# FFN products at full array width, and the first batch's outputs stored by SyncE from the accumulators' buffers

## The chip, the cores and the metric

The kernel runs on one core of a Trainium2 chip. A core has a matrix engine (TensorE, PE in the profile; its weight loads have a row of their own, PEld), three engines for element-wise work (VectorE or DVE, ScalarE or ACT, GpSimd or POOL), and SyncE (SP), which only issues transfers. ACT and POOL issue transfers as well. Each engine works through its own list of instructions in order; engines wait for each other, and for transfers, by semaphores.

The metric is the device time of one execution in microseconds. Seven executions of the kernel before lie between 547.52 and 553.15 us, with a median of 549.8 us.

## What is computed

Attention with squared ReLU in place of softmax, followed by a layer norm and a two-layer feed-forward part (FFN) with a residual:

```python
scores = scale * np.matmul(q, k.transpose(0, 1, 3, 2))      # q, k, v: 8 batches, 12 heads, 448 tokens, 64
attn = np.maximum(scores, 0.0) ** 2 / S
attn_out = np.matmul(attn, v)
x = attn_out.transpose(0, 2, 1, 3).reshape(B, S, H * D)      # 8 x 448 x 768
xn = (x - mu) / np.sqrt(var + 1e-06) * g_ln
ch = np.maximum(xn @ w_ch1, 0.0) @ w_ch2                    # 768 -> 3072 -> 768
out = x + ch
```

## The kernel before

**Order of the work.** All instructions are issued in an order that is written out by hand; nothing reorders them. Batch 0's attention comes first, in fine steps (step_fine, L531). Then, for each batch b, FFN 1 (ffn_1_all, L587) and FFN 2 (ffn_2_first, L616, for batch 0, and ffn_2_all, L642, for the others). The attention of batch b + 1 is spread over the FFN of batch b: in batch 0 by step_a and step_b, later in groups called excursions (L513): one attention value product if one is due, then two or three score products with their ReLU and square, and then the FFN goes on.

**Products.** A matmul has a stationary side of up to 128 columns and a moving side. Scores (L225) contract over the 64 elements of a head, two heads in the two halves of the array's rows. The value product (att_AV, L250) has 64 stationary columns a head and puts two heads into the two halves of the array's columns, as the transposes of batches 0 and 1 (pe_T, L189) do. Their stationary sides are shown as 64*112, 112*64 and 112*64.

FFN 1 (ffn_1, L317) makes 128 of the 3072 hidden features at a time for a batch's 448 tokens: six contraction steps, each of which is two matmuls of 64 stationary columns (128*64), one for either half of the columns. Only the first three feature tiles of batch 0 (ffn_1_first, L568, matmuls on L574) use 128 columns at once. Results go to two PSUM banks in turn (next_f), and ACT writes their ReLU to h (L324). FFN 2 of batch 0 (plain_part, L358) takes two token tiles of 128 and two halves of 384 output features, each in four parts of six contraction steps; every step is again a pair of 64-column matmuls (L367). FFN 2 of the other batches (seven, L395) makes two token tiles at a time with seven products of half size (Strassen's way), by product (L381, matmuls on L384), from sums of pieces of h (s_sb, L378) and of w2 (w2_sums, L174). center (L278) takes the mean of x by a matmul with constants, in pairs as well (L282).

**Around batch 0's FFN 2.** Between its sixteen parts ACT scales x of batch 1 by the gains (gain, L276), DVE subtracts the mean (center_part, L288), copies the tokens left over to the next batch (carry, L333) and makes sums of w2 (L176). After a tile's last part DVE adds the residual (scaled_plus, L353) into a buffer of o_pool (new_o, three buffers), and the result is stored. store (L339) makes two transfers of one tile, as a tile's 128 tokens cross a boundary of 112 in the output's layout. It takes the issuing engines as an argument: SP if none is named, and for batch 0 ACT. The other batches' outputs are in buffers of o_pool and of acc_pool (four buffers, tag "acc"), and SP stores them.

**SP's list.** SP also issues the transposes of q and k for the batches from 2 on (att_T, L202: two for each pair of heads; three pairs' results fit into t_pool) and the transposes of x into x_tok, tokens on the rows (ffn_x, L300). At the end of batch 0 its list is: six transposes of q and k (pairs 12 to 14), then twelve of x for batch 1, with those of pair 15 after the sixth and of pair 16 after the twelfth.

Of the kernel before, what the change touches and what calls it, by code (L numbers as in the profile page):

```python
# [11 lines left out]
def kernel(  # L12
# [10 lines left out]
    nc = tc.nc  # L23
    P = 128
    bf16 = mybir.dt.bfloat16
    fp32 = mybir.dt.float32
# [3 lines left out]
    B, H, S, D = q.shape  # L30
# [8 lines left out]
    K1 = d_model // P  # L39
    K2 = d_ff // P  # L40
    KH = K2 // 2
    HD = d_model // 2
# [14 lines left out]
    acc_pool = ctx.enter_context(tc.tile_pool(name="acc", bufs=4))  # L57
# [9 lines left out]
    ones = const_pool.tile([P, P], bf16)  # L67
# [5 lines left out]
    w1 = big_pool.tile([P, K1, d_ff], bf16)  # L73

    w2 = big_pool.tile([P, 7, KH, HD], bf16)
    B11, B22, B12, B21, B_SUM, B_TOP, B_BOT = range(7)
    h = big_pool.tile([P, K2, HW], bf16)
# [3 lines left out]
    xc = big_pool.tile([P, K1, S], bf16)  # L81
# [158 lines left out]
    def xT_of(b, ki):  # L240
        return xT[:, ki, (b % 2) * S:(b % 2 + 1) * S]
# [36 lines left out]
    def center(b):  # L278
        mean_ps = spare[1][:, :S]
        for n, part in enumerate((xs, xT_of(b, K1 - 1))):  # L280
            for c in range(2):
                nc.tensor.matmul(mean_ps[c * D:(c + 1) * D, :], ones[:, :D], part,  # L282
                                 start=(n == 0), stop=(n == 1))
        for ki in range(K1):
            center_part(ki, mean_ps)

    def center_part(ki, mean_ps):
        nc.vector.scalar_tensor_tensor(xc[:, ki, :], mean_ps, g_sb[:, ki:ki + 1], xc[:, ki, :],  # L288
                                       op0=Alu.mult, op1=Alu.add)
# [27 lines left out]
    def ffn_1(ni):  # L317
        ps = next_f()[:, :S]
        for ki in range(K1):
            for c in range(2):  # L320
                n0 = ni * P + c * D
                nc.tensor.matmul(ps[c * D:(c + 1) * D, :], w1[:, ki, n0:n0 + D], xc[:, ki, :],  # L322
                                 start=(ki == 0), stop=(ki == K1 - 1))
        nc.scalar.activation(h[:, ni, CARRY:], ps, Act.Relu)  # L324

    def h_cols(b, m):
        c0 = CARRY + m * P - b * S
        return slice(c0, c0 + P)
# [6 lines left out]
    def new_o():  # L335
        o_t = o_pool.tile([P, HD], fp32, tag="o")
        return o_t

    def store(o_t, m, d0, d1, engines=(nc.sync,)):  # L339
        c0 = m * P  # L340
        n = 0
        while c0 < (m + 1) * P:
            g0 = c0 // SP
            c1 = min((m + 1) * P, (g0 + 1) * SP)
            bb, jj = divmod(g0, NJ)
            engines[n % len(engines)].dma_start(
                out_tok[bb, c0 - g0 * SP:c1 - g0 * SP, jj, d0:d1],
                o_t[c0 - m * P:c1 - m * P, :d1 - d0])
            c0 = c1
            n += 1  # L350

    def scaled_plus(o_t, y, m, plus):
        nc.vector.scalar_tensor_tensor(o_t, y, rstd[:, m:m + 1], plus, op0=Alu.mult, op1=Alu.add)  # L353

    def x_half(m, dh):
        return x_tok[:, m % NT, dh * HD:(dh + 1) * HD]

    def plain_part(b, m, dh, part, parts, box):  # L358
        if part == 0:
            box[0] = next_f()[:, :HD]  # L360
        n = K2 // parts
        cols = h_cols(b, m)
        for ki in range(part * n, (part + 1) * n):
            slot = ((B11, B12), (B21, B22))[ki // KH][dh]
            for c in range(2):
                t0 = cols.start + c * D
                nc.tensor.matmul(box[0][c * D:(c + 1) * D, :], h[:, ki, t0:t0 + D],  # L367
                                 w2[:, slot, ki % KH, :], start=(ki == 0), stop=(ki == K2 - 1))
        if part == parts - 1:
            o_t = new_o()  # L370
            scaled_plus(o_t, box[0], m, x_half(m, dh))
            store(o_t, m, dh * HD, (dh + 1) * HD, (nc.scalar,))

    s_turn = Turns(range(4))

# [4 lines left out]

    def product(ps, stat, slot, start, d0=0, d1=HD):  # L381
        for ki in range(KH):
            for c in range(2):
                nc.tensor.matmul(ps[c * D:(c + 1) * D, :d1 - d0], stat[:, ki, c * D:(c + 1) * D],  # L384
                                 w2[:, slot, ki, d0:d1],
                                 start=(start and ki == 0), stop=(ki == KH - 1),
                                 skip_group_check=not start)

    posts = []

# [4 lines left out]
    def seven(b, pair, banks, last, between):  # L395
# [43 lines left out]
        def s(name, x, y, op):  # L439
# [3 lines left out]

        steps = [
            (lambda: product(c, a11, B12, True), s(1, a11, a22, Alu.add), after3),
            (lambda: product(d, a22, B21, True), s(5, a11, a12, Alu.add), after4),
            (lambda: product(a, sums[1], B_SUM, True), s(2, a21, a22, Alu.add), after1),
            (lambda: product(c, sums[5], B22, False), s(7, a12, a22, Alu.subtract), after5),
            (lambda: product(d, sums[2], B11, False), s(6, a21, a11, Alu.subtract), after2),
# [137 lines left out]
    def ffn_1_all(b):  # L587
        steps = second_steps() if b == 0 else None
        ms = tiles_of(b)
        for ni in range(3 if b == 0 else 0, K2):  # L590
            if b == 0 and ni == 3:
                ffn_1_first()
            if 3 <= ni < 3 + K1:
                ffn_x(b, ni - 3)
            ffn_1(ni)
            flush()
            m = (ni - (K2 - 2 * len(ms))) // 2
            if m >= 0 and ni % 2 == 0:
                ffn_stats(ms[m])
            if b == 1 and ni in SUMS_AT:  # L600
                w2_sums(*LATE_SUMS[SUMS_AT.index(ni)])
            if b == 0 and ni % 2 == 1:
                next(steps)()
            if 0 < b < B - 1 and ni in IN_FFN1[b]:
                excursion(3, relus=(2,))
        assert steps is None or next(steps, None) is None
# [9 lines left out]
    def ffn_2_first():  # L616
        b = 0
        ffn_rstd(b)
        box = {}
        n = 0  # L620
        for dh in range(2):
            for m in range(2):
                for part in range(4):
                    plain_part(b, m, dh, part, 4, box)
                    if n == 1:
                        att_AV(PE_T * NPAIR - 1, bank=spare[0])
                    if n < K1 - 1:
                        gain(1, n)
                    if n == 3:
                        gain(1, K1 - 1)  # L630
                    if n == 4:
                        gain(1, K1 - 2)
                        center(1)
                    if n == 8:
                        carry(b)
                    if n in (9, 10):
                        w2_sums(B_SUM, B11, B22, Alu.add, n - 9)
                    if n in (12, 13):
                        w2_sums(B_TOP, B11, B12, Alu.add, n - 12)
                    n += 1  # L640

    def ffn_2_all(b):  # L642
# [9 lines left out]
        def between(n):  # L652
            n += 7 * (pr - first)
            if n == (8 if len(pairs) == 2 else 1):
                carry(b)
            if b == B - 1:
                return
            if slots_left():
                if n in (1, 3):
                    excursion(min(2, slots_left()), av_bank, nc.scalar, square_by=nc.scalar)  # L660
            elif ready:
                att_AV(ready.pop(0), bank=av_bank, evac_by=nc.scalar)
            done = (b + 2) * NPAIR - len(ready) - NPAIR * (b + 1)
            done -= sum(1 for i, t in slots if t == NJ - 1 and i < (b + 2) * NPAIR)
            if not gains and not centered[0]:
                center(b + 1)
                centered[0] = True
            for _ in range(2):
                if gains and gains[0] < done:
                    gain(b + 1, gains.pop(0))  # L670
# [75 lines left out]
```

## Time and profile before

One execution was profiled. It took 552.49 us; its span, from the first to the last instruction, is 550.6 us.

| | before |
|---|---|
| median of seven executions | 549.8 us |
| the profiled execution | 552.49 us |
| its span | 550.6 us |
| instructions | 13785 |
| matmuls, and as many weight loads | 5729 |
| FFN 1 matmuls in pairs (L322) | 2268, of 448 columns |
| FFN 2 matmuls in pairs (L384, L367) | 2208 and 192, mostly of 384 columns |
| granted TensorE clock, mean | 0.994 |

A row of the profile's groups names the line, engine and operation, then what is written and read, the stationary side (128*64: 128 rows, 64 columns), the moving side, the count, the busy time and the mean duration, and last the idle time of the engine before the group with what ended it. Matmuls overlap: a matmul of 448 columns is shown 350 to 355 ns long, while the next one can start about 190 ns after it, so the time of a stream is read from starts. In the timeline a row is "start, duration, engine, line", with equal instructions joined, and in brackets how long the engine was idle ahead of it and what ended that. The row PEclk gives the granted clock in 40 slices of 13.8 us each.

### The profile page before, as it was taken

Reading aid. Unit: us, or ns where it says so; the run is one execution under the profiler, and the core shown is the slowest. Engines: PE = TensorE matmul, PEld = TensorE weight load, DVE = VectorE, ACT = ScalarE, POOL = GpSimd, SP = SyncE. Lnnn points to the kernel's source line nnn. Section 1 sums busy time; section 2 is a strip of 40 time slices with the busy share of each in tenths; the row PEclk is TensorE's granted clock in tenths of the full one; section 3 lists DMA queues with packets and bytes.
Section 4 is the critical chain, followed back from the end, with each engine's and each line's share of the span. In section 5 each row is a group of like instructions: output and inputs, shape, how many; then the busy total and the mean of one; then the engine's idle time right before and its main releaser. Section 6 shows DMA issues by size and latency. Waiting matters only on the chain. (4 is left out here: it accounts for less than half of the span.)

```text
span 550.6 us, 13785 instructions
## 1 busy us (share of the span) xinstructions
PE 528.9 (96%) x5729; PEld 342.6 (62%) x5729; DVE 369.4 (67%) x660; ACT 306.6 (56%) x487; POOL 205.0 (37%) x261
## 2 busy tenths in 40 slices
PE   7999997799999999999999999999999999999996
PEld 4445565355786556855578556654578556787785
DVE  4975668499584785757866679766866678740464
ACT  6957741565816666266662765376562766524421
POOL 7421137036444642445524438224815200240021
PEclk9999999799999999999999999999999999999999
DMA  9999999669536984269942789258942820122022
GB/s 153 195 188 207 204 170 149 87 88 107 63 67 105 113 83 69 62 104 108 94 69 64 79 91 133 54 85 87 125 69 73 92 35 3 30 79 57 11 59 59
DMA packets 163022, 51.87 MB, mean 94 GB/s; under 512 B 128784, under 2 KB 162960, under 8 KB 162960
## 3 DMA queue, kind: packets, MB, share of 16 engines
q0 software_dynamic: 94208, 25.74, 48.2%
q1 hardware_dynamic: 67616, 24.07, 24.0%
q10 hardware_dynamic: 1136, 1.19, 0.7%
q8 instruction: 45, 0.74, 0.6%
q14 instruction: 17, 0.14, 0.1%
HBM read 51.91 MB, written 11.01 MB: 114 GB/s over the span
## 5 line engine op out<-in xcount | busy, mean ns | idle before, releaser
L322 PE MATMUL f<-xc,w 128*64 128x448 bf16 x2268 | 227.7, 355 | 6.2 <-ACT h L324 3.3
L322 PEld LDWEIGHTS <-w 128*64 128x64 bf16 x2268 | 131.1, 110 | 94.9 <-issue 23.7
L324 ACT ACTIVATE h<-f 128x448 bf16<-128x448 f32 x189 | 103.0, 545 | 100.5 <-PE f L322 86.4
L231 ACT ACTIVATE at<-sc 112x896 bf16<-112x896 f32 x149 | 128.3, 916 | 16.1 <-PE sc L225 15.9
L384 PE MATMUL f<-w,s_sb 128*64 128x384 bf16 (+2 forms) x1584 | 132.6, 324 | 1.2 <-DVE s_sb L378 1.2
L384 PEld LDWEIGHTS <-s_sb 128*64 128x64 bf16 x1584 | 103.8, 110 | 25.8 <-issue 2.7
L236 DVE TENSOR_TENSOR at<-at 112x896 bf16<-112x896 bf16 x177 | 100.9, 618 | 7.6 <-ACT at L231 7.4
L136 POOL DMA_DIRECT2D qk_ring<-in_q_dram x72 | 50.8, 711 | 112.0 <-DMA qkT_t<-qk_ring 91.7
L418 POOL TENSOR_TENSOR o_t<-o_t,x_tok 128x384 f32<-128x384 f32 x26 | 23.8, 914 | 138.9 <-ACT o_t L417 84.9
L229 DVE TENSOR_SCALAR at<-f 112x448 bf16<-112x448 f32 x86 | 49.5, 617 | 35.9 <-PE f L225 35.9
L378 DVE TENSOR_TENSOR s_sb<-h 128x1536 bf16<-128x1536 bf16 x65 | 63.3, 991 | 0.0
L136 POOL DMA_DIRECT2D qk_ring<-in_k_dram x72 | 50.3, 703 | 18.8 <-DMA w<-in_moe_w_ch_dram 12.4
L384 PE MATMUL f<-w,h 128*64 128x384 bf16 x624 | 54.3, 326 | 2.3 <-DVE acc L432 1.8
L418 POOL TENSOR_TENSOR acc<-acc,x_tok 128x384 f32<-128x384 f32 x25 | 35.8, 1442 | 42.4 <-ACT acc L417 42.4
L384 PEld LDWEIGHTS <-h 128*64 128x64 bf16 x624 | 40.9, 110 | 13.6 <-issue 3.8
L225 PE MATMUL sc<-qkT_t 64*112 64x448 bf16 x298 | 47.0, 378 | 1.5 <-DMA qkT_t<-qk_ring 1.2
L417 ACT ACTIVATE o_t<-f,rstd 128x384 f32<-128x384 f32 x26 | 14.9, 575 | 54.7 <-DVE acc L422 38.0
L260 DVE TENSOR_SCALAR xT<-f 128x448 bf16<-128x448 f32 x37 | 22.8, 617 | 30.2 <-PE f L250 20.6
L288 DVE SCALAR_TENSOR_TENSOR xc<-f,g_sb,xc 128x448 bf16<-128x448 f32 x48 | 29.3, 677 | 19.3 <-PE f L282 15.0
L250 PE MATMUL f<-at,v_ring 112*64 112x448 bf16 x336 | 41.0, 354 | 0.1
L225 PEld LDWEIGHTS <-qkT_t 64*112 64x112 bf16 x384 | 20.1, 126 | 33.4 <-issue 26.9
L417 ACT ACTIVATE acc<-acc,rstd 128x384 f32<-128x384 f32 x25 | 14.8, 610 | 34.8 <-DVE acc L432 33.4
(65 smaller groups left out, 342.6 us busy)
## 6 DMA issues: line engine op xcount, KB each, us to landing
w<-in_moe_w_ch_dram POOLq DMA_DIRECT2D x6, 768.0 KB, 27.7
w<-in_moe_w_ch_dram POOLq DMA_DIRECT2D x4, 1152.0 KB, 36.5
qk_ring<-in_q_dram POOLq DMA_DIRECT2D x72, 56.0 KB, 3.4
qk_ring<-in_k_dram POOLq DMA_DIRECT2D x72, 56.0 KB, 3.9
v_ring<-in_v_dram POOLq DMA_DIRECT2D x36, 112.0 KB, 4.0
out_dram<-o_t SPq DMA_DIRECT2D x7, 168.0 KB, 2.2
x_tok<-xT SPq DMA_TRANSPOSE x72, 3.6
qkT_t<-qk_ring SPq DMA_TRANSPOSE x72, 3.3
```

The lines of the kernel that those rows point to most:

```text
L136: nc.gpsimd.dma_start(sb[:, :, x, :], src[b, 2 * a + x].rearrange("(p j) d -> p j d", j=NJ))
L225: nc.tensor.matmul(half[:SP, :S], qkT[i][r, 1, t * SP:(t + 1) * SP], qkT[i][r, 0, :], start=True, stop=True)
L229: nc.vector.tensor_scalar(at[:, hh], spare[hh][:SP, :S], 0.0, None, op0=Alu.max)
L231: nc.scalar.activation(at, ps[:SP, :, :S], Act.Relu)
L236: nc.vector.tensor_mul(attn[i, t], attn[i, t], attn[i, t])
L250: nc.tensor.matmul(ps[hh * D:(hh + 1) * D, :], v_of(i)[:, hh, t * D:(t + 1) * D], attn[i, t][:, hh, :], start=(t == 0), stop=(t == NJ - 1))
L322: nc.tensor.matmul(ps[c * D:(c + 1) * D, :], w1[:, ki, n0:n0 + D], xc[:, ki, :], start=(ki == 0), stop=(ki == K1 - 1))
L324: nc.scalar.activation(h[:, ni, CARRY:], ps, Act.Relu)
L378: nc.vector.tensor_tensor(s_sb[:, n], x, y, op=op)
L384: nc.tensor.matmul(ps[c * D:(c + 1) * D, :d1 - d0], stat[:, ki, c * D:(c + 1) * D], w2[:, slot, ki, d0:d1], start=(start and ki == 0), sto ...
L417: nc.scalar.activation(o_t, y, Act.Identity, scale=rstd[:, m:m + 1])
L418: nc.gpsimd.tensor_tensor(o_t, o_t, x_half(m, dh), op=Alu.add)
```

## The change

There are two parts. The FFN products and the mean of center run with 128 stationary columns in one matmul where two matmuls of 64 stood. Batch 0's four output tiles are put into acc_pool's buffers in place of o_pool's, and are stored by SP in place of ACT. On SP the eight stores then stand after the six transposes of pairs 12 to 14 and before those of x for batch 1.

```diff
 def center(b):
     mean_ps = spare[1][:, :S]
     for n, part in enumerate((xs, xT_of(b, K1 - 1))):
-            for c in range(2):
-                nc.tensor.matmul(mean_ps[c * D:(c + 1) * D, :], ones[:, :D], part,
-                                 start=(n == 0), stop=(n == 1))
+            nc.tensor.matmul(mean_ps, ones, part, start=(n == 0), stop=(n == 1))
...
 def ffn_1(ni):
     ps = next_f()[:, :S]
     for ki in range(K1):
-            for c in range(2):
-                n0 = ni * P + c * D
-                nc.tensor.matmul(ps[c * D:(c + 1) * D, :], w1[:, ki, n0:n0 + D], xc[:, ki, :],
-                                 start=(ki == 0), stop=(ki == K1 - 1))
+            nc.tensor.matmul(ps, w1[:, ki, ni * P:(ni + 1) * P], xc[:, ki, :],
+                             start=(ki == 0), stop=(ki == K1 - 1))
...
 def plain_part(b, m, dh, part, parts, box):
...
-            for c in range(2):
-                t0 = cols.start + c * D
-                nc.tensor.matmul(box[0][c * D:(c + 1) * D, :], h[:, ki, t0:t0 + D],
-                                 w2[:, slot, ki % KH, :], start=(ki == 0), stop=(ki == K2 - 1))
+            nc.tensor.matmul(box[0], h[:, ki, cols], w2[:, slot, ki % KH, :],
+                             start=(ki == 0), stop=(ki == K2 - 1))
         if part == parts - 1:
-            o_t = new_o()
+            o_t = acc_pool.tile([P, HD], fp32, tag="acc")
             scaled_plus(o_t, box[0], m, x_half(m, dh))
-            store(o_t, m, dh * HD, (dh + 1) * HD, (nc.scalar,))
+            store(o_t, m, dh * HD, (dh + 1) * HD)
...
 def product(ps, stat, slot, start, d0=0, d1=HD):
     for ki in range(KH):
-            for c in range(2):
-                nc.tensor.matmul(ps[c * D:(c + 1) * D, :d1 - d0], stat[:, ki, c * D:(c + 1) * D],
-                                 w2[:, slot, ki, d0:d1],
-                                 start=(start and ki == 0), stop=(ki == KH - 1),
-                                 skip_group_check=not start)
+            nc.tensor.matmul(ps[:, :d1 - d0], stat[:, ki], w2[:, slot, ki, d0:d1],
+                             start=(start and ki == 0), stop=(ki == KH - 1),
+                             skip_group_check=not start)
```

## The prediction

> **What bounds the kernel now.** I read the page's busy shares and clock row first, then the chain of waits that ended last, then the waits of 70 to 125 us, then the timeline there.
>
> ```profile
> PE 528.9 (96%) x5729; PEld 342.6 (62%) x5729; DVE 369.4 (67%) x660; ACT 306.6 (56%) x487; POOL 205.0 (37%) x261
> ...
>
> ```
>
> ```profile
> 491.13 27.24 PE f L322 x288
> ```
>
> TensorE is the bound: 528.9 of 550.6 us busy, and the last chain is nearly all matmuls. The second fence is one piece of that chain: 288 matmuls of 64 columns are 144 pairs in 27.24 us, so **189.2 ns a pair** of 448 columns. Two halves run beside each other; a pair is not two times 189 ns. So almost every time that I remove from TensorE counts, and almost nothing that I remove elsewhere. One clock digit is not 9: slice 7 (96 to 110 us).
>
> ```profile
> ACT h L324 <- DMA out_dram<-o_t: 13.4, 1, 13.4
> ...
> ACT xc L276 <- DMA qkT_t<-qk_ring: 7.8, 1, 7.8
> ...
> PE f L322 <- ACT h L324: 3.3, 1, 3.3
> ```
>
> ```profile
> 87.67 4.09 PE L367 MATMUL f<-w,h 128*64 128x384 bf16 x48 [1.97 <-DVE o_t L353]
> ...
> 95.16 1.33 PE L322 MATMUL f<-xc,w 128*64 128x448 bf16 x12 [1.74 <-DVE o_t L353]
> ...
> 99.22 0.98 ACT L324 ACTIVATE h<-f 128x448 bf16<-128x448 f32 x2 [13.44 <-DMA out_dram<-o_t]
> 99.81 2.45 PE L322 MATMUL f<-xc,w 128*64 128x448 bf16 x12 [3.32 <-ACT h L324]
> ...
> 102.20 0.99 PE L225 MATMUL sc<-qkT_t 64*112 64x448 bf16 x4
> ```
>
> The first of these two fences is the table of waits in that window (who waited <- for what: us, times, longest), the second the timeline. Eight stores of batch 0 are issued by ACT (L372). ACT works in order, so a store whose wait isn't over holds everything behind it. The second store waits, by the semaphore it carries, for an earlier DMA of the same semaphore, one of SP's transposes; ACT's gains (L276) stand behind it for 7.8 us. DVE's centring waits for these gains, and the second output (L353) stands behind the centring; PE needs its bank: 1.97 us. The other stores hold ACT until 99.22, so that the first ReLUs of batch 1 are 13.4 us late: 3.32 us of PE.
>
> **Part 1: the stores go to SP.** What the stall costs. PE idle is 1.97 + 0.34 (at 92.10) + 1.74 + 3.32 = 7.37 us. A matmul's row ends some 0.16 us after the next could have started (350 ns long at a pitch of 189), so each of the four gaps in the stream is longer by that: +0.65. After the last gap the clock is low: the windows give 0.58 for 96 to 100 us and 0.56 for 100 to 104. There 12 matmuls take 2.45 us that take 1.33 at 95.16 (+1.1), and the scores that start at 102.20 are followed by FFN work at 103.49, 1.29 us later, where the next such group takes 0.70 (107.02 to 107.72): +0.6. Sum 9.7 us. (The Trainium skill, "TensorE: Matmul & The Clock Gate", section "Why this matters for your kernels", has the clock fall after a PE gap of some 3 us; the 3.32 us gap with 0.56 after it agrees, so without the gap the digit should be 9.)
>
> What is late next. With ACT free, its six gains are done by 77.6 us and the centring runs 78.98 to 82.7 (six at 0.62). Then DVE in its order: second output 0.6 (to 83.4), carry 1.45, two weight sums 2.6, third output 0.6 (88.0), two sums 2.6, fourth output (91.2). PE with no gap ends the sixteen parts at about 89.4, the first FFN 1 group at 90.6, and the second needs the bank that the fourth output frees: about 0.7 us of wait stays. **Gain 9.0 us.** The last w2 load lands at 78.6 us (issued 40.0, 38.6 to landing), before its first use at some 84, so loads don't take the gain.
>
> What the stores cost on SP. In SP's list the eight stand behind the six qkT transposes that end at 91.5 us, and in front of batch 1's twelve x_tok transposes and the qkT pair of heads 15, then 16. An issue is 0.34 us, and each waits for the DMA eight before it, here the last qkT transposes, landing at 94 to 95. So x_tok starts near 95.8 instead of 91.55, and SP goes on at 1.28 us a transpose: six to 103.5, two qkT to 106, six to 113.8, then the qkT of pair 16, landing at 117 to 119.5. PE wants it where it stood at 126.45, less 9, about 117.5. That is a wait of 0 to 2 us which was not there: **+1.0**. The x_tok readers (L313, 127.06 before) come later than that.
>
> A rule that speaks against expecting anything here: the skill's front page ("Trainium Kernel Development and Optimization", "Key Constraints") says that issuing DMAs from several engines saves only the sequencer's issue time. By it the move gives 8 x 0.34 = 2.7 us of ACT, all of it beside PE: nothing. The rows show 21 us of ACT standing behind waits that the issue carries, 9.7 of it passed on to PE. I take the rows.
>
> The tiles: batch 0 takes the four acc buffers, each once, so the fourth output no longer waits for a store of the first (3 o buffers, 4 outputs). The next user of acc is batch 1's FFN 2, near 136 us, 35 us after the stores: nothing.
>
> **Part 2: full width.** Removed: half of 2268 (L322), 2160 + 48 short ones (L384), 192 (L367) and 28 (L282) matmuls with their weight loads. PE streams the same columns.
>
> ```profile
> 32.13 0.73 PE L574 MATMUL f<-xc,w 128*128 128x448 bf16 x3 [0.78 <-DVE xc L288]
> ```
>
> ```profile
> 28.98 0.36 PE L273 MATMUL f<-xT,ones 128*128 128x448 bf16 x1
> 29.18 0.38 PE L477 MATMUL f<-w,ones 128*128 128x256 bf16 x2
> 29.49 0.79 PE L250 MATMUL f<-at,v_ring 112*64 112x448 bf16 x4
> ```
>
> ```profile
> 206.33 0.82 PE L384 MATMUL f<-w,h 128*64 128x384 bf16 x8
> 206.98 0.93 PE L250 MATMUL f<-at,v_ring 112*64 112x448 bf16 x8
> ```
>
> Three timelines of PE. L574 is the same product at full width already: three matmuls in 0.73 us, less one length of 0.35, are two pitches of **0.19 us**, as a pair (finer starts give 188.4 ns against 189.2). Its weight loads last 96 ns and lie wholly beside the matmuls. Gain 0 to 0.8 ns for each of 2310: 0 to 1.8 us, I take 0.8.
>
> The price is elsewhere: the attention value products (L250) and transposes (L189) stay at 64 columns. In the third timeline eight matmuls, four pairs of 0.162, start 0.65 us before L250: no gap at the boundary. In the second, two full-width matmuls of 256 columns (pitch 0.109) are followed by 64-column ones 0.31 us after their start: 0.31 - 0.22 = **0.09 us** lost. That is what the skill's "TensorEngine Tiling (Array Packing)", "Key Properties", states: a change of tiling mode drains the array. The 64-row scores (L225) pay it already on both sides. New are the boundaries FFN to L250 (25 + 12), L250 to FFN (9) and L189 to FFN (5), counted in the timeline of the matmuls: 51 x 0.093 = **+4.8 us**. Returns: after a switch a pair's second start is 24 ns late, a full-width one's 11, at 57 returns from the scores: -0.7; the stagger of a pair before the scores (4 to 31 ns, 34 times): -0.5. At the end, 12 matmuls of 128 columns run at 56 ns a pair with loads of 96 to hide: 0 to +0.5, I take +0.3.
>
> On the rule that speaks against this part: "TensorE: Matmul & The Clock Gate", "The mechanism", says a weight load overlaps running matmuls only where the row group differs. All full-width matmuls share their rows; by it each would add its 96 ns, 2310 x 0.096 = +222 us. L574 shows no such addition; I take the row.
>
> Part 2: -0.8 + 4.8 - 0.7 - 0.5 + 0.3 = **+3.1 us** (ends +1.5 and +5).
>
> **Sum.** -9.0 + 1.0 + 3.1 = **-4.9 us** on a span of 550.6, whose execution took 552.5; the runs' median is 549.8, so 544.9. Ends by terms: -9.7 + 0 + 1.5 = -8.2 (541.6) and -7.5 + 2 + 5 = -0.5 (549.3).
>
> **Rivals.**
> - *The switches hide.* For: several boundaries already wait for a bank, and the 0.09 rests on the small products of batch 0. Then only part 1 counts: -8.5, 541. Chance 0.2.
> - *SP takes ACT's place.* The twelve x_tok transposes behind the stores push each qkT of batch 1 so late that PE waits at each group of scores, not at one: another 4 us given back, 549. For: SP would be busy without a break from 79 to 119. Against: it had free time from 100.5 to 107.4. Chance 0.15.
> - *Slower: weight loads come out from cover* in the 384-column products, where 96 ns has to fit into 162 and no full-width row of before has that shape. Price: x ns for each of 1176 in FFN 2. Below 4 ns the sum still ends under 549.8; from 7 ns on it is slower by over 0.5%; a load exposed by 10 ns gives 557. Against: the 256-column L477 keeps 109 ns with the same load. Chance 0.1.
> - *The change doesn't do what it says*: the moved stores still hold ACT through shared semaphores. ACT then has no DMA left to issue in that stage, so only its own waits for data remain; I give it nothing.
>
> **How the numbers follow.** Forecast 544.9, chance 0.55. A measurement here can tell about 0.5% (2.7 us) from no change. Faster by more: 0.5 of the forecast's 0.55, all of the first rival, a little of the second, 0.72. Same: the rest of these, 0.16. Slower: the third and what I haven't seen, 0.12. Range 540.5 to 549: the forecast, the first rival and the near half of the second.
>
> **What would show it.** ACT's waits of 7.8 and 13.4 us gone; PE digits 9 in slices 6 and 7, clock 9 everywhere; the scores that stood at 102.20 near 93.3; FFN 1 of the last batch at 188 to 189 ns a matmul (24 groups in 27.2 us); 0.28 us instead of 0.19 from an FFN matmul's start to L250. Wrong would be: a pitch above 192 or 165 ns, PE waiting for qkT by more than 2 us, or the stall replaced by one on SP.

## The result, and the profile after

| | before | after |
|---|---|---|
| median | 549.93 us (31 executions, 547.09 to 553.15) | 545.60 us (12 executions, 544.36 to 546.97) |
| the profiled execution | 552.49 us, span 550.6 | 544.73 us, span 543.0 |
| instructions, matmuls among them | 13785, 5729 | 9112, 3381 |

The ratio is 0.9916, with a 95% interval of 0.9897 to 0.9936: 4.3 us less. The two profiled executions differ by 7.6 us of span, more than the medians do. The times of the kernel before spread over 6 us and its profiled execution lies in their upper part, so that what is read from the two traces alone is somewhat too large.

The page after, its engine row and its clock row:

```profile
PE 531.3 (98%) x3381; PEld 274.3 (51%) x3381; DVE 369.2 (68%) x660; ACT 305.4 (56%) x487; POOL 203.8 (38%) x261
...
PEclk9999999999999999999999999999999999999999
```

TensorE is busier, 98% of a shorter span, and no slice of the clock row is below 9. Before, slice 7 was a 7:

```profile
PEclk9999999799999999999999999999999999999999
```

The timeline after, in the stage where the stall was:

```profile
76.53 1.93 ACT L276 ACTIVATE xc<-xT,g_sb 128x448 bf16<-128x448 bf16 x3 [0.43 <-DVE xT L260]
...
82.91 0.61 DVE L349 SCALAR_TENSOR_TENSOR o_t<-f,rstd,x_tok 128x384 f32<-128x384 f32 x1
...
87.24 4.75 SPq L342 DMA_DIRECT2D out_dram<-o_t  x8
...
89.80 3.81 PE L318 MATMUL f<-xc,w 128*128 128x448 bf16 x18
...
93.54 0.58 PE L225 MATMUL sc<-qkT_t 64*112 64x448 bf16 x4
...
94.25 3.58 PE L318 MATMUL f<-xc,w 128*128 128x448 bf16 x18
```

The gains are done by 78.5 us, the second output starts at 82.91 (87.00 before), and FFN 1 of batch 1 (L318 now) runs its first three feature tiles in one piece of 18 matmuls: none of the three gaps is left. A little of the wait for the fourth output is still inside that piece: its 18 matmuls are shown 3.81 us long, the next 18 (at 94.25 us) 3.58. The first scores of batch 1 start at 93.54 us instead of 102.20, and 8.7 us are won at this point. From here to the end the changed kernel loses a little again. Its chain of waits that ended last (start, length, what):

```profile
483.52 27.24 PE f L318 x144
510.76 27.34 PE f L377 x180
```

The same FFN 1 stood at 491.13 us before, 7.6 us later. So 1.1 us of the 8.7 was given back in between. The length of 27.24 us is the same to the hundredth, with 144 matmuls in place of 288. So is that of FFN 2 behind it, which was this before:

```profile
518.37 27.34 PE f L384 x360
```

Where it was given back is seen at the borders of the value products. A window of PE's timeline after, and one of the same place before:

```profile
101.12 0.92 PE L318 MATMUL f<-xc,w 128*128 128x448 bf16 x4
101.97 0.95 PE L250 MATMUL f<-at,v_ring 112*64 112x448 bf16 x8
```

```profile
110.40 0.92 PE L322 MATMUL f<-xc,w 128*64 128x448 bf16 x8
111.15 0.93 PE L250 MATMUL f<-at,v_ring 112*64 112x448 bf16 x8
```

Four pitches of 0.189 us are 0.76. After, the value product starts 0.85 us after the first of four matmuls, so 0.09 us is lost. Before it starts 0.75 us after the first of four pairs, and nothing is lost.

One wait works the other way and hides a part of this. In batch 5 the kernel before waits for a transpose of q or k, and so does the run of the stores alone, below (1.12 us); the changed kernel has no such wait.

```profile
384.15 0.40 PE L225 MATMUL sc<-qkT_t 64*112 64x448 bf16 x2 [1.20 <-DMA qkT_t<-qk_ring]
```

### The profile page after: what moved, and what is told of

Same layout as the page of the kernel before. It is cut to its first block, busy times and chain, and to the rows that moved or that the text cites. A ratio compares the mean times of both kernels' runs of the same rounds, so it can differ in the third digit from the quotient of the medians.

```text
span 543.0 us, 9112 instructions
## 1 busy us (share of the span) xinstructions
PE 531.3 (98%) x3381; PEld 274.3 (51%) x3381; DVE 369.2 (68%) x660; ACT 305.4 (56%) x487; POOL 203.8 (38%) x261
## 5 line engine op out<-in xcount | busy, mean ns | idle before, releaser
L318 PE MATMUL f<-xc,w 128*128 128x448 bf16 x1134 | 225.3, 353 | 0.8 <-DVE xT L260 0.5
L318 PEld LDWEIGHTS <-w 128*128 128x128 bf16 x1134 | 106.6, 98 | 111.5 <-issue 17.9
L320 ACT ACTIVATE h<-f 128x448 bf16<-128x448 f32 x189 | 103.0, 545 | 98.3 <-PE f L318 84.9
L377 PE MATMUL f<-w,s_sb 128*128 128x384 bf16 (+1 forms) x792 | 131.8, 324 | 1.2 <-DVE s_sb L372 1.2
L377 PEld LDWEIGHTS <-s_sb 128*128 128x128 bf16 x792 | 75.8, 98 | 53.5 <-issue 2.7
L377 PE MATMUL f<-w,h 128*128 128x384 bf16 x312 | 53.8, 326 | 2.1 <-DVE acc L424 1.5
L377 PEld LDWEIGHTS <-h 128*128 128x128 bf16 x312 | 30.4, 98 | 23.9 <-issue 3.9
```

Source lines behind the costliest of these rows:

```text
L318: nc.tensor.matmul(ps, w1[:, ki, ni * P:(ni + 1) * P], xc[:, ki, :], start=(ki == 0), stop=(ki == K1 - 1))
L377: nc.tensor.matmul(ps[:, :d1 - d0], stat[:, ki], w2[:, slot, ki, d0:d1], start=(start and ki == 0), stop=(ki == KH - 1), skip_group_check= ...
```

## The experiments

The kernel before ran beside them each time; its median was 550.07 us in the first group of four, 550.29 in the next three and 548.20 beside the last two.

### The stores alone, and the width alone

Two kernels undo one half of the change each. The first has the stores on SP from acc's buffers, with all products in pairs as before. Against the kernel before, its edit is:

```diff
-            o_t = new_o()
+            o_t = acc_pool.tile([P, HD], fp32, tag="acc")
             scaled_plus(o_t, box[0], m, x_half(m, dh))
-            store(o_t, m, dh * HD, (dh + 1) * HD, (nc.scalar,))
+            store(o_t, m, dh * HD, (dh + 1) * HD)
```

> The change's stores (SP issues them, acc buffers), all FFN products still in pairs of 64 columns. Theory A (the stores give all of the gain, full width costs about 50 changes of array mode at 0.093 us less what it returns, some 2 to 4 us): faster than the changed kernel, 541.5 to 543.5 us, FFN matmul to value product 0.185 us in the stream instead of 0.28. Rival B (the gain comes from the full width, with half the matmuls and weight loads): like the kernel before, 549 to 550 us. Rival C (both parts give some): 546 to 549.

Measured: 542.43 us (ratio to before 0.9874, 0.9849 to 0.9899), and 542.84 us when it ran a second time, for which this was expected:

> The stores alone a second time, beside the run with the later transposes of x, on the same chip. All theories: 541.9 to 543.2 us, as the first time.

Its last FFN 1, from the chain of waits that ended last:

```profile
480.78 27.24 PE f L322 x288
```

The stores give 7.6 us (550.07 - 542.43), more than the whole change does; beside the second run, where the kernel before had 548.20, they give 5.4. Full width on top of them costs 3.2 us (545.60 - 542.43; 2.8 by the second run). Theory A holds, B and C fall. This kernel is faster than both.

The traces of the changed kernel and of the stores alone show where the cost lies. From the start of one batch's FFN 1 to the next, full width is 0.9 us longer in batch 0 and 0.51 to 0.56 us in batches 1 to 4 and 6. In batch 5 it is 0.8 us shorter, as its wait for q or k is missing. Without that the cost would be about 4 us, an estimate from these stretches. Why the wait is missing isn't known.

The second has full width and the stores as they were. Its edit, like those of the runs that follow unless it is said otherwise, is against the changed kernel:

```diff
-            o_t = acc_pool.tile([P, HD], fp32, tag="acc")
+            o_t = new_o()
             scaled_plus(o_t, box[0], m, x_half(m, dh))
-            store(o_t, m, dh * HD, (dh + 1) * HD)
+            store(o_t, m, dh * HD, (dh + 1) * HD, (nc.scalar,))
```

> Full width alone; batch 0's stores stay on ACT with o_pool's buffers. Theory A: slower than the kernel before by 2 to 4 us, 552 to 554 us, ACT's waits of some 8 and 13 us still there. Rival B: 545 to 546, as the changed kernel. Rival C: 547 to 549.

Measured: 550.71 us, ratio 1.0026 (0.9999 to 1.0053). It is not faster, so B and C fall here too, but it is 0.6 us slower, not 2 to 4. Its timeline:

```profile
87.93 4.06 PE L361 MATMUL f<-w,h 128*128 128x384 bf16 x24 [1.55 <-DVE o_t L349]
...
95.55 4.08 PE L318 MATMUL f<-xc,w 128*128 128x448 bf16 x12 [1.77 <-DVE o_t L349]
96.40 0.54 ACT L320 ACTIVATE h<-f 128x448 bf16<-128x448 f32 x1 [10.36 <-DMA out_dram<-o_t]
```

PE waits for outputs as in the kernel before, but ACT comes free at 96.40 us instead of 99.22, and the 3.32 us gap for its ReLU is missing. The cost of full width and a shorter stall nearly cancel. The granted clock of the single executions shows the same. Where its mean over an execution was 0.999 or more, the kernel before has a median of 548.16 us (13 of 58 executions beside these runs) and this one 551.04 (5 of 12), 2.9 us more. A mean under 0.996 befell 29 of the 58 (median 551.03), and 2 of the 12. Whether full width itself makes the longest gap rarer isn't settled.

The clock falls in this run too, though no wait of PE is above 1.77 us: it was 0.63 from 96 to 100 us, and slice 7 of the row shows it.

```profile
PEclk9999999899999999999999999999999999999999
```

### The four buffers

```diff
-            o_t = acc_pool.tile([P, HD], fp32, tag="acc")
+            o_t = new_o()
```

> The changed kernel with batch 0's tiles back in o_pool's three buffers, still stored by SP. Theory A: the fourth output has to wait for the first tile's two stores, which land at 92.4 us in the changed kernel's trace, while the fourth output began at 90.5: DVE is held about 1.9 us and PE's second FFN 1 group of batch 1 with it, so 1 to 2 us slower, 546.5 to 547.5. Rival D (the buffers don't matter, only the issuing engine): within 0.5 us of the changed kernel.

Measured: 548.90 us, 3.3 us slower than the changed kernel, and spread as the kernel before is (545.47 to 551.97). Rival D falls, and theory A has the direction but half the size or so. Its timeline, first at the fourth output and then in batch 5:

```profile
92.49 0.62 DVE L349 SCALAR_TENSOR_TENSOR o_t<-f,rstd,x_tok 128x384 f32<-128x384 f32 x1 [1.96 <-DMA out_dram<-o_t]
...
93.16 2.43 PE L318 MATMUL f<-xc,w 128*128 128x448 bf16 x12 [1.98 <-DVE o_t L349]
```

```profile
378.94 0.40 PE L225 MATMUL sc<-qkT_t 64*112 64x448 bf16 x2 [0.96 <-DMA qkT_t<-qk_ring]
```

With three buffers the fourth output waits 1.96 us for the landing of the first tile's stores, and PE waits 1.98 us behind it. A second wait, of 0.96 us, is the one of batch 5 again. It is no result of the buffers as far as the traces show: SP does start the transposes of x for batch 1 later (93.98 us instead of 92.12), but PE has no wait for q or k in batch 1, the kernel before has the same wait in batch 5 with other stores, and counted from the start of that batch's FFN 1 SP issues its last transpose of x at 21.7 us here as in the changed kernel. So the buffers account for 2.0 us in this trace; what the rest of the 3.3 us between the medians is stays open.

The same buffers with the stores on ACT:

```diff
-            store(o_t, m, dh * HD, (dh + 1) * HD)
+            store(o_t, m, dh * HD, (dh + 1) * HD, (nc.scalar,))
```

> The changed kernel with the eight stores back on ACT, but in acc's four buffers. Theory A (with ACT held, DVE is so late that the fourth output finds its buffer free anyway; in the run of full width alone it began at 94.89 us, when the first tile's second store had landed at 88.5): the buffers bring nothing here, 550 to 551.5 us, as full width alone. Rival (the four buffers bring their 3.3 us with any issuing engine): 547 to 548.

Measured: 550.71 us, the time of full width alone. The buffers bring nothing while ACT is held, and 3.3 us by the medians once it isn't. Its timeline shows the way from the gains to PE:

```profile
85.63 2.49 ACT L276 ACTIVATE xc<-xT,g_sb 128x448 bf16<-128x448 bf16 x4 [8.90 <-DMA qkT_t<-qk_ring]
...
90.00 4.06 PE L361 MATMUL f<-w,h 128*128 128x384 bf16 x24 [2.76 <-DVE o_t L349]
```

PE's waits for outputs are 2.76, 0.49 and 1.77 us here, and it has none for the ReLU: the late gains alone carry the loss (the lower clock that follows, 0.67 from 100 to 104 us, included).

### Which stores hold ACT

The next two split the stores: the first tile's on ACT and the rest on SP, and the other way round.

```diff
-            store(o_t, m, dh * HD, (dh + 1) * HD)
+            store(o_t, m, dh * HD, (dh + 1) * HD, (nc.scalar,) if m + dh == 0 else (nc.sync,))
```

> The changed kernel with only the first tile's two stores on ACT. Theory A (most of the loss comes from the gains that stand behind the first tile's second store, by way of the centring and the later outputs on DVE): ACT held some 5 to 8 us from 78.5 us on, PE waits of 1.5 + 0.5 + 1.8 us for outputs return, 549 to 550.5 us. Rival (the loss is the first ReLUs of batch 1 behind the last stores): 545.5 to 546.5, as the changed kernel.

Measured: 545.53 us, as the changed kernel. Theory A falls as I wrote it; the rival's number came out, but not for its reason:

```profile
77.98 1.04 ACTq L342 DMA_DIRECT2D out_dram<-o_t  x2
...
79.08 2.49 ACT L276 ACTIVATE xc<-xT,g_sb 128x448 bf16<-128x448 bf16 x4 [4.12 <-issue]
```

Both stores are issued within 1.04 us and the gains follow at once. Before, the two took 5.03 us:

```profile
78.21 5.03 ACTq L346 DMA_DIRECT2D out_dram<-o_t  x2
```

The semaphores that the trace records with each transfer tell why. In these traces the transfers of SP and ACT carry eight semaphores in turn (100, 102 and 113 to 118 in the records, 0 to 7 here), and one that finds its semaphore in use waits for the landing of the transfer that had it. The first tile's two stores, and SP's first transpose of q or k there:

```
before     ACT  store 1: number 0   store 2: number 1    SP  first transpose: number 1
this one   ACT  store 1: number 7   store 2: number 0    SP  first transpose: number 1
```

Before, the second store and the transpose share number 1, and the store waits for that transpose to land (at 82.90 us; the store is issued at 82.92). Here numbers 7 and 0 were last used by transfers that had landed by 37 us. So a store on ACT isn't slow as such: it holds ACT when its turn of the semaphores falls on a transfer of SP that is late itself. PE does wait 0.77 us for the fourth output in this trace; the medians don't show it.

```diff
-            store(o_t, m, dh * HD, (dh + 1) * HD)
+            store(o_t, m, dh * HD, (dh + 1) * HD, (nc.sync,) if m + dh == 0 else (nc.scalar,))
```

> The changed kernel with the first tile's stores on SP and the other three tiles' six stores on ACT. Theory A: the gains are in time, so DVE's outputs keep their times, and only the first ReLUs of batch 1 stand behind ACT's stores: 546 to 548.5 us. Rival (the ReLUs are the larger part of the loss): 549 to 551.

Measured: 552.81 us, ratio 1.0054 (1.0028 to 1.0080), slower than every other form of the stores. Theory A falls, the rival's direction holds beyond its number.

```profile
85.27 12.91 ACTq L342 DMA_DIRECT2D out_dram<-o_t  x6
...
98.23 0.98 ACT L320 ACTIVATE h<-f 128x448 bf16<-128x448 f32 x2 [19.46 <-DMA x_tok<-xT]
98.82 2.40 PE L318 MATMUL f<-xc,w 128*128 128x448 bf16 x6 [6.20 <-ACT h L320]
```

The gains and all outputs are in time (the fourth output at 90.67 us), and yet ACT is held to 98.2 us by transposes that share the stores' semaphores: one of q or k, which lands at 92.88 us, then two of x (95.75 and 97.56), each followed within 0.1 us by the store. PE waits 6.20 us in one piece, and its clock falls: 0.50 from 98 to 102 us, and 2.40 us for six matmuls that take 1.3. So either of the two ways, the late gains or the late ReLUs, costs all of the stall by itself.

### The price of a change of array mode

```diff
-            nc.tensor.matmul(ps, w1[:, ki, ni * P:(ni + 1) * P], xc[:, ki, :],
-                             start=(ki == 0), stop=(ki == K1 - 1))
+            for c in range(2) if ni % 2 else ():
+                n0 = ni * P + c * D
+                nc.tensor.matmul(ps[c * D:(c + 1) * D, :], w1[:, ki, n0:n0 + D], xc[:, ki, :],
+                                 start=(ki == 0), stop=(ki == K1 - 1))
+            if ni % 2 == 0:
+                nc.tensor.matmul(ps, w1[:, ki, ni * P:(ni + 1) * P], xc[:, ki, :],
+                                 start=(ki == 0), stop=(ki == K1 - 1))
```

> The changed kernel with every second feature tile of FFN 1 in pairs of 64 columns and the others at full width; the same columns are streamed, and the array changes its mode 361 times instead of 233. Theory A (a change of mode costs 0.093 us wherever it is): 128 x 0.093 = 11.9 us slower than the changed kernel, 556.5 to 558.5. Rival (the 0.093 us at the borders of value products belongs to these products, not to the change of mode): within 1 us of the changed kernel, as pairs and full width have the same pitch of 189.2 ns.

Measured: 558.85 us, 13.25 us more than the changed kernel, for 128 more changes of mode: **0.104 us each**, a little above theory A's range. The chain in the last batch's FFN 1, where no value product is near:

```profile
494.51 1.13 PE f L323 x6
495.65 1.26 PE f L320 x12
496.90 1.24 PE f L323 x6
```

Six matmuls of full width after the same mode take 1.13 us, after the other mode 1.24 (L323), and six pairs 1.26 (L320), where six pairs in a row take 1.14 (a 24th of 27.24). The 0.11 to 0.12 us belongs to the change of mode, in either direction, and not to the value products. The rival falls.

### Later transposes of x

In the run of the stores alone PE waited 1.4 us for transposes of q and k, which SP issues behind those of x. So the latter were moved to later feature tiles from batch 1 on, in the kernel of the stores alone:

```diff
-            if 3 <= ni < 3 + K1:
-                ffn_x(b, ni - 3)
+            x0 = 3 if b == 0 else 8
+            if x0 <= ni < x0 + K1:
+                ffn_x(b, ni - x0)
```

> The stores alone (products in pairs, SP stores from acc's buffers), and from batch 1 on the transposes of x are issued from FFN 1's ninth feature tile instead of its fourth. Theory A (SP, which issues one transpose in 1.28 us, makes PE wait 1.4 us for the transposes of q and k in the run of the stores alone, 0.3 of it in batch 1 and 1.1 in batch 5): about 1 us faster than the stores alone, 541 to 542 us, if the token statistics don't then wait for x. Rival (SP has room, these waits come from the loads of q and k): within 0.3 us of it, 542.1 to 542.7.

Measured: 560.47 us, 18 us slower than the stores alone. Neither theory had this. Its timeline in batch 5:

```profile
378.05 0.62 DVE L260 TENSOR_SCALAR xT<-f 128x448 bf16<-128x448 f32 x1 [3.51 <-DMA x_tok<-xT]
...
378.73 2.46 PE L322 MATMUL f<-xc,w 128*64 128x448 bf16 x24 [1.62 <-DVE xT L260]
```

The next batch's value product is written into xT by DVE, and DVE waits 3.51 us until the transposes have read xT. DVE's squares stand behind it, and PE behind both; the longest waits of PE, for the squares, are 4.70 and 3.17 us, and after each the clock is at 0.50 for some 4 us. Both theories asked who waits for the transposes' results, and not who waits for what they read.

## Why the prediction was right

Forecast 544.9 us, measured 545.60; -4.9 us forecast, -4.3 measured. The mechanism is the one forecast: the stores held ACT, their move removes the stall, and full width takes a part back. That the sum came within 0.6 us is partly luck, as two of its terms were off in opposite directions: the stall by 1.4 us and SP by 1.0. Point by point:

- *What the stall costs, -9.0.* The path is right, the size belongs to the profiled execution. There the first scores stand 9.7 us earlier with the stores alone (92.51 in place of 102.20), 0.5 of which comes from ahead of batch 0's FFN 1. But that execution lies in the upper part of its kernel's times; by the medians the stores alone give 7.6 us, and 5.4 in the second run. In the changed kernel the scores were expected near 93.3 us and stand at 93.54. The explanation by ACT's order and the shared semaphores is what the split stores show; that either of two ways costs the whole stall wasn't foreseen.
- *The wait of 0.7 us that stays* for the fourth output is 0.24: the second group's first matmul starts 0.43 us after the one ahead of it, at 91.18 us, where the pitch is 0.19.
- *The tiles.* I gave the four buffers one sentence and no number of their own. They are worth 3.3 us of the stores' 7.6 by the medians, 2.0 of it seen in the trace, and without them the range of the kernel before would be back.
- *SP, +1.0.* It measured 0 in the changed kernel. I took the end of the six transposes of q and k from the trace of before, 91.5 us. In the changed kernel SP is done with them at 87.1 us and starts x at 92.12, not 95.8. At the place that I named, the run of the stores alone waits 0.31 us (116.65 us), and its repetition not at all. The waits of 1.0 to 1.5 us for q or k in the other traces are in batch 5, and the kernel before has one too.
- *Full width, +3.1.* Measured 3.2 and 2.8, with two small terms wrong. The pitch gains nothing (27.24 us for 144 as for 144 pairs), where I had -0.8 from 18 matmuls of L574; and the tail costs nothing (27.34 us as before), where I had +0.3. The price of a change of mode, 0.093, measured 0.09 to 0.11. The wait in batch 5, which the changed kernel lacks, takes about 1.3 us off the cost; it was in no term, so the close number is partly luck here too.
- *The clock.* I tied its fall to the one gap of 3.32 us. That is too narrow: with full width alone it fell to 0.63 after waits of 1.55, 0.50 and 1.77 us within 8 us, while the single wait of 1.98 us (o_pool's buffers) left it at 1.00. How much idle time it takes isn't measured here.
- *The rules.* The row decided each time. The drain at a change of mode, which the Trainium skill states in "TensorEngine Tiling (Array Packing)", "Key Properties", costs 0.104 us here. The sentence in "TensorE: Matmul & The Clock Gate", "The mechanism", by which a weight load overlaps matmuls only on other rows, isn't borne out: 144 full-width matmuls, each with its load, take the 27.24 us of 144 pairs. The same section also lets a load into the background weight buffer go ahead of running matmuls, which I passed over and which agrees. That only issue time is saved by another issuing engine (the skill's "Trainium Kernel Development and Optimization", "Key Constraints") falls short here, as the two splits (545.53 and 552.81 us) show.
- *The rivals.* That the switches hide is refuted by the alternating kernel; that SP takes ACT's place by the lack of any wait for SP's transposes in the changed kernel; that the loads come out from cover by the equal 27.34 us.

## What to carry to other kernels

An engine that computes should not issue a transfer whose wait isn't over: its price is everything behind it in that engine's list, and the semaphore on which it waits can be that of another engine's transfer, handed out in turn, so that moving one transfer changes who is held. Two column tiles of the array streamed as fast as the full width here, so full width had nothing to gain and cost what changes of mode it added: count the borders with the work that keeps the other mode, at about 0.1 us each. A trace shows one execution; where a kernel's times spread, see where the profiled one lies before its stall is taken off the median. When a transfer is moved, look at who waits to overwrite what it reads as well as at who waits for what it writes.

## What the hardware showed unexpectedly

At the very end 12 matmuls of 128 columns run with full weight loads. The weight loads' timeline after:

```profile
537.26 0.60 PEld L377 LDWEIGHTS <-s_sb 128*128 128x128 bf16 x10
```

Ten loads, each shown 98 ns long, take 0.60 us together: (0.60 - 0.098) / 9 is one every 56 ns, which is the pitch of the matmuls there, and of the pairs before. So the rows of loads overlap each other: the length shown is not the time that must pass until the next load, and here the loads don't limit the array even at 128 columns.
